# Attention, routed experts and a two-layer net: sink values loaded compactly and spread on chip, value maxima listed for ScalarE first

## The chip, the cores and the metric

The kernel runs on one core of one Trainium2 chip. The metric is the device time of one execution in microseconds (us), lower is better. Engines are named as in the profile: PE is TensorE (matmul), DVE is VectorE, ACT is ScalarE, POOL is GpSimd, SP is SyncE, which here only issues DMAs.

## The reference

Three stages follow one another. The first is attention with a sliding window of 128 keys and 4 "sink" keys, which every query sees:

```python
B, H, S, D = 2, 8, 768, 64
scores = scale * np.matmul(q, k.transpose(0, 1, 3, 2))
keep = is_sink | in_window
scores = np.where(keep, scores, -1000000000.0)
scores = scores - np.max(scores, axis=-1, keepdims=True)
a = np.exp(scores)
a = a / (np.sum(a, axis=-1, keepdims=True) + 1e-09)
return np.matmul(a, v).astype(np.float32)
```

The second routes 1536 tokens to 8 experts, 192 each, by a greedy order over all logits, and applies the expert's two layers (512 to 1024 to 512, with a relu). The third applies two dense layers (512 to 2048 to 512) with a leaky slope per column.

## The kernel before

**Planner.** The kernel does not write its instructions in the order of the loops. It lists tasks: each has an estimated duration for every engine that may run it, what it reads and what it writes. `Plan.run` then places them one after another: the task that can start first, and among those that can start together the one with the longest way to the end. Each engine runs its instructions in the order that comes out, so an instruction that waits on the chip holds up all that stands behind it on its engine. Where a task may run on two engines, the first one named is preferred: the other takes it only if it would be done earlier by a margin (`bias`, 0.85 us unless given). A changed estimate or preference can therefore move instructions anywhere in the stage.

**Attention.** Twelve blocks of 128 queries (6 per batch), each with four pairs of heads. For a pair: PE computes scores for two key blocks and four sink columns (line 485). DVE adds the mask and takes the row's extreme in one custom instruction (line 495, once per head). ACT takes the exponential into tile P (line 506, once per head). PE transposes P (line 520). ACT casts the transposed P to a 16-bit high part (line 529) and DVE subtracts it to get the low part (line 530). PE multiplies both with the values, which are also kept as a high part vh and a low part vl (lines 571 to 575). DVE divides by the row sums (lines 598 to 603).

**The values.** Four DMAs of three blocks each bring them to tile vraw. They are split in 16 bits after a scaling by a power of two, found from the largest absolute value over the six blocks of a batch. `vmax` takes the maximum of a block: on ACT as the sum of absolute values (line 407, an upper bound that serves as well), on DVE as a reduction (line 409). `BY_ACT` lists the blocks whose task names ACT first; for the others DVE is first. Behind six maxima stands a short chain of DVE and PE steps (`pow2_scale`, lines 388 to 396), which gives the scale svf. Only then can vh and vl be made, and only then can the first values product start.

**The sink values.** PE multiplies the probabilities of the sinks (tile sk, made by POOL at lines 539 to 541) with tile vsh, whose row for head h holds values only in the columns of head h and zeros elsewhere. Before the change that layout, zeros and all, is loaded from memory: vsr, 96 partitions by 2 x 2 x 8 x 65 numbers. `prep_vs` scales a batch of it on ACT (lines 454 and 455) and subtracts the high part on DVE in the low-part rows (line 458), over 1024 columns each time.

**Loads.** One queue on SP brings all inputs. `ORDER` names the order of the early ones: k and q of block 1, values a and b (blocks 0 to 2 and 3 to 5), the sink values s, the gate's weights w. The keys and queries of the later blocks and the other values follow.

**The end of the stage.** For each block the gate's logits are computed; the order of the 1536 tokens is then counted by comparing every token's best logit with every other's. The comparisons (tiles cm) are differences written by ACT (line 1121) or POOL (line 1123) and turned to 0 or 1 by DVE (lines 1127 and 1131), or made by DVE alone (line 1116). Blocks 0 to 8 are one group, blocks 9 to 11 a second, whose broadcast of logits (mrow, line 1100) needs the last block. PE sums them (line 1163), and the first expert follows. Everything from there on hangs on the end of that count.

## Time and profile before

| | us |
|---|---|
| median of 3 runs | 609.66 |
| lowest and highest of them | 609.23, 613.13 |
| the profiled execution, whole time | 608.75 |
| its span on the core | 607.0 |

The profile is of one execution. The span runs from its first to its last instruction; 1.75 us of its time lie around it. The attention stage with the count of tokens takes the first 119 us of the span. "Busy" is time in which an engine has at least one instruction; idle time is put down to what ended it. In rows by line, the mean is of one instruction, and instructions that overlap on an engine count once in its busy time.

### The profile page before, as it was taken

The page shows a single profiled execution, that of the slowest core. Times are in us where ns is not written, and L with a number is a line of the kernel's source. Part 1 is how long each engine was busy: PE and PEld are TensorE (multiplying, and loading weights), DVE is VectorE, ACT ScalarE, POOL GpSimd, SP SyncE. Part 2 cuts the span into 40 slices and gives each one's busy share as a digit, 9 for nine tenths or more (in the row PEclk, how much of TensorE's full clock was granted, in tenths as well). Part 3 has the DMA queues.
Part 4 walks back from the last instruction along what each step waited for, and adds up shares of the span by engine and source line. Part 5 has one row for each costly group of instructions (what it writes and reads, how often), then busy time and mean ns, then how long its engine had stood idle before and what let it go on. Part 6 is the DMA issues. An engine that isn't in the chain of part 4 may idle for free.

```text
span 607.0 us, 12432 instructions
## 1 busy us (share of the span) xinstructions
PE 559.9 (92%) x4532; PEld 410.0 (68%) x4532; DVE 461.2 (76%) x1299; ACT 357.7 (59%) x742; POOL 161.0 (27%) x247
## 2 busy tenths in 40 slices
PE   5899997659789999999899999999999999899995
PEld 3567675449688668888898555598755559855552
DVE  6989987858647898998699998989987657743231
ACT  6778888357457967866665553566344446542222
POOL 4867835230643321436301201000220000020002
PEclk9789998569889999999999999999999999999998
DMA  8845354264868536343554448464697155210001
GB/s 282 295 104 134 100 87 140 50 219 116 305 183 280 205 105 209 97 138 107 153 164 157 131 144 309 164 195 153 196 321 256 39 169 166 80 43 10 1 0 53
DMA packets 40555, 91.99 MB, mean 152 GB/s; under 512 B 16703, under 2 KB 17230, under 8 KB 40398
## 3 DMA queue, kind: packets, MB, share of 16 engines
q1 hardware_dynamic: 37710, 84.27, 44.3%
q0 software_dynamic: 2784, 6.93, 3.3%
q8 instruction: 36, 0.59, 0.4%
q14 instruction: 25, 0.20, 0.1%
HBM read 82.15 MB, written 6.41 MB: 146 GB/s over the span
## 4 chain that ended last, share of the span: by engine, by line
PE 47%; issue 12%; DVE 11%; ACT 8%; DMA 4%; POOL 1%; another core or an unknown queue 0%; POOLq 0%; SPq 0%; ACTq 0%
PE o L1751 14%; PE h L1708 13%; PE h L1574 8%; PE h L1581 8%; DMA xg<-xd,sidx 3%; DVE spl L1559 1%; DVE cm L1116 1%; PE r L1163 1%; DVE cm L1131 1%; ACT w L860 1%; PE r L1459 1%; ACT spl L1557 1%; ACT cm L1121 1%; DVE w L900 1%; DMA L<-cd 1%
## 5 line engine op out<-in xcount | busy, mean ns | idle before, releaser
L1751 PE MATMUL o<-w,gt 128*128 128x512 f16 x432 | 101.9, 379 | 0.0
L1708 PE MATMUL h<-x,w 128*128 128x384 f16 x576 | 100.7, 326 | 0.0
L1708 PEld LDWEIGHTS <-w 128*128 128x128 f16 x576 | 55.8, 98 | 40.6 <-issue 0.5
L1721 ACT ACTIVATE t<-h,slope 128x384 f32<-128x384 f32 x64 | 37.0, 578 | 72.3 <-PE h L1708 72.2
L1751 PEld LDWEIGHTS <-gt 128*128 128x128 f16 x432 | 41.3, 98 | 43.3 <-issue 0.5
L1581 PEld LDWEIGHTS <-spl 128*128 128x128 f16 x768 | 63.4, 98 | 3.2 <-issue 2.6
L1724 DVE SCALAR_TENSOR_TENSOR v<-h,way,t 128x384 f32<-128x384 f32 x61 | 37.3, 612 | 35.3 <-ACT t L1721 35.3
L907 POOL TENSOR_TENSOR w<-w,sg 128x512 f32<-128x512 f32 x22 | 28.8, 1310 | 88.8 <-DVE w L900 29.0
L1574 PE MATMUL h<-xT,raw 128*128 128x192 f32 x256 | 48.1, 338 | 2.3 <-DVE x L1625 1.8
L1446 POOL DMA_INDIRECT xg<-xd,sidx x16 | 20.6, 1286 | 100.5 <-DVE sidx L1440 62.4
L1574 PE MATMUL h<-h,raw 128*128 128x192 f32 x256 | 46.4, 339 | 0.4 <-DVE x L1625 0.4
L506 ACT ACTIVATE P<-sm,mn 128x260 f32<-128x260 f32 (+1 forms) x96 | 42.7, 491 | 4.7 <-DVE mn L495 4.6
L1797 POOL DMA_INDIRECT out<-ot,sidx x9 | 8.9, 990 | 136.2 <-ACT ot L1788 97.4
L1574 PEld LDWEIGHTS h<-xT,raw 128*128 128x128 f32 x256 | 42.5, 194 | 3.4 <-DVE x L1625 2.1
L1574 PEld LDWEIGHTS h<-h,raw 128*128 128x128 f32 x256 | 43.5, 198 | 1.1 <-DVE x L1625 0.6
L1559 DVE SCALAR_TENSOR_TENSOR spl<-raw,es,spl 128x1024 f16<-128x1024 f32 x32 | 40.7, 1280 | 4.5 <-ACT spl L1557 4.4
L1728 ACT CAST gt<-v 128x384 f16<-128x384 f32 x48 | 24.5, 510 | 28.9 <-DVE v L1724 27.5
L485 PE MATMUL s<-k,q 64*128 64x260 f32 (+1 forms) x192 | 36.8, 457 | 4.4 <-DMA q<-qT 4.1
L495 DVE CUSTOM_DVE_ANT_0 sm<-s,mask 128x260 f32<-128x260 f32 (+1 forms) x96 | 35.7, 397 | 4.1 <-PE s L485 3.8
L1729 DVE TENSOR_TENSOR gt<-v,gt 128x384 f16<-128x384 f32 x48 | 26.5, 553 | 13.7 <-ACT gt L1728 13.6
L1557 ACT ACTIVATE spl<-raw,es 128x1024 f16<-128x1024 f32 x32 | 36.4, 1143 | 0.0
L1581 PE MATMUL h<-xT,spl 128*128 128x192 f16 x384 | 33.5, 246 | 1.5 <-DVE h L1604 1.2
(291 smaller groups left out, 1241.5 us busy)
## 6 DMA issues: line engine op xcount, KB each, us to landing
raw<-w SPq DMA_DIRECT2D x96, 512.0 KB, 4.6
r<-w_in SPq DMA_DIRECT2D x16, 512.0 KB, 8.1
r<-w_out SPq DMA_DIRECT2D x16, 512.0 KB, 4.4
vraw<-v SPq DMA_DIRECT2D x4, 768.0 KB, 8.5
xd<-x SPq DMA_DIRECT2D x12, 256.0 KB
k<-kT SPq DMA_DIRECT2D x11, 260.0 KB
q<-qT SPq DMA_DIRECT2D x11, 256.0 KB, 2.8
vsr<-vs SPq DMA_DIRECT2D x1, 780.0 KB
```

Of the source, the lines that this page charges most:

```text
L485: nc.tensor.matmul(s.tile[:, :n].rearrange("p (j k) -> p j k", k=KW), lhsT=qs[t].tile[half, p], rhs=kk, start=True, stop=True)
L495: task({"DVE": dve(n)}, lambda: nc.vector.tensor_tensor_reduce(out=sm.tile[:, :n], in0=s.tile[:, :n], in1=mask[:, :n], scale=-0.125, scala ...
L506: task({"ACT": act(n) + 0.137}, lambda h=h, sm=sm, mn=mn: nc.scalar.activation(P[t].tile[:, h, :n], sm.tile[:, :n], AF.Exp, bias=mn.tile, ...
L907: (nc.gpsimd if e == "POOL" else nc.vector).tensor_tensor(x.tile, x.tile, sg.tile, OP.mult)
L1557: task({"ACT": act_sb(1024) + 0.09}, lambda: nc.scalar.activation(v(0), src(), AF.Copy, scale=scale()), r=[raw, ws], w=[b.part(0)], lag=se ...
L1559: task({"DVE": dve(1024) + 0.2}, lambda: nc.vector.scalar_tensor_tensor(v(1), src(), scale(), v(0), OP.mult, OP.subtract), r=[raw, ws, b.p ...
L1574: nc.tensor.matmul(ps.tile[:, 0:CAP], lhsT=w[:, k], rhs=x, start=first and k == 0, stop=last and k == 3, skip_group_check=True)
L1581: nc.tensor.matmul(ps.tile[:, 0:CAP], lhsT=w[:, i, k], rhs=xs()[k][:, j], start=first and n == 0, stop=last and n == len(ways) - 1, skip_g ...
L1708: nc.tensor.matmul(ps.tile[:, 0:CH], lhsT=w[:, i, k], rhs=y[j][:, k], start=(n == 0), stop=(n == len(ways) - 1))
L1721: task({"ACT": act(CH)}, lambda: nc.scalar.activation(t.tile, ps.tile[:, 0:CH], AF.Copy, scale=slope), r=[ps, wres], w=[t])
L1724: task({"DVE": dve(CH) + 0.065}, lambda: nc.vector.scalar_tensor_tensor(to(), ps.tile[:, 0:CH], way, t.tile, OP.mult, OP.max), r=[ps, t, w ...
L1751: nc.tensor.matmul(ops[t].tile, lhsT=gv[:, i, sl], rhs=wv[:, j], start=(f == n == 0), stop=(f == FB - 1 and n == 2))
```

## The change

Three things are done. `ORDER` puts the gate's weights ahead of the sink values. `BY_ACT` names all twelve blocks, so that each maximum has ACT as its preferred engine. The sink values come as vsr without the head dimension (96 x 260 numbers, 97.5 KB in place of 780 KB), are scaled and split at that size into vsd (ACT over 128 columns, DVE over 128), and are then spread over the heads by one multiplication of 96 x 1040 with a 0 or 1 mask named own; that task may run on POOL or on DVE. The mask is a reduction of the identity matrix on DVE.

```diff
--- before.py
+++ after.py
@@ -247,9 +247,9 @@
 TURNED = 2
 URGENT = 10.0
 EAGER = 40.0
-ORDER = "k q a b s w"
+ORDER = "k q a b w s"
 LATER = {2: (6, 9), 3: (9, 12)}
-BY_ACT = (0, 1, 3)
+BY_ACT = tuple(range(12))
 BIG = 1.0e30
 
 
@@ -292,7 +292,9 @@
     vraw = cst.tile([128, NBLK, DM], F32, name="vraw")
     kall = cst.tile([128, B, NB, NP, KW], F32, name="k")
     wgs = cst.tile([128, NP, E], F32, name="wgs")
-    vsr = cst.tile([96, B, 2, H, D + 1], F32, name="vsr")
+    vsr = cst.tile([96, B, 2, D + 1], F32, name="vsr")
+    vsd = cst.tile([96, B, 2, D + 1], F16, name="vsd")
+    own = cst.tile([96, H], F16, name="own")
     vsh = cst.tile([96, B, 2, H, D + 1], F16, name="vsh")
     wg16 = cst.tile([128, 2, NP, E], F16, name="wg16")
     mx = cst.tile([128, NBLK], F32, name="mx")
@@ -333,7 +335,7 @@
         load(lambda: nc.sync.dma_start(out=wgs, in_=wg), [wg_res], 1 << 14)
 
     def load_vs():
-        load(lambda: nc.sync.dma_start(out=vsr, in_=vs), [vs_res], 1 << 19)
+        load(lambda: nc.sync.dma_start(out=vsr, in_=vs), [vs_res], 1 << 17)
 
     for x in ORDER.split():
         {"a": lambda: load_v(0, 3), "b": lambda: load_v(3, 6), "c": lambda: load_v(6, 9), "d": lambda: load_v(9, 12),
@@ -345,6 +347,9 @@
         if t in LATER:
             load_v(*LATER[t])
 
+    own_res = Res()
+    task({"DVE": 0.2}, lambda: nc.vector.tensor_reduce(
+        own, ident[0:96, 0:96].rearrange("p (r h x) -> p h r x", r=3, h=H), AX.XY, OP.max), w=[own_res])
     warm = cst.tile([128, 1], F32, name="warm")
     nc.vector.memset(warm, 0.0)
     nc.scalar.activation(warm, warm, AF.Exp)
@@ -451,13 +456,22 @@
 
     def prep_vs(b):
         def first():
-            nc.scalar.activation(vsh[:, b, :, :, 0:D], vsr[:, b, :, :, 0:D], AF.Copy, scale=svf[b][0:96])
-            nc.scalar.copy(vsh[:, b, :, :, D:D + 1], vsr[:, b, :, :, D:D + 1])
-
-        task({"ACT": 1.1}, first, r=[vs_res, sv_res[b]], w=[vsh_res[b]])
-        task({"DVE": 1.15}, lambda: nc.vector.scalar_tensor_tensor(
-            vsh[64:96, b, :, :, 0:D], vsr[64:96, b, :, :, 0:D], svf[b][64:96], vsh[64:96, b, :, :, 0:D],
-            OP.mult, OP.subtract), r=[vs_res, sv_res[b]], w=[vsh_res[b]])
+            nc.scalar.activation(vsd[:, b, :, 0:D], vsr[:, b, :, 0:D], AF.Copy, scale=svf[b][0:96])
+            nc.scalar.copy(vsd[:, b, :, D:D + 1], vsr[:, b, :, D:D + 1])
+
+        def rest():
+            nc.vector.scalar_tensor_tensor(vsd[64:96, b, :, 0:D], vsr[64:96, b, :, 0:D], svf[b][64:96], vsd[64:96, b, :, 0:D],
+                                           OP.mult, OP.subtract)
+
+        def spread(e):
+            (nc.vector if e == "DVE" else nc.gpsimd).tensor_tensor(
+                vsh[:, b], vsd[:, b].unsqueeze(2).to_broadcast([96, 2, H, D + 1]),
+                own.unsqueeze(1).unsqueeze(3).to_broadcast([96, 2, H, D + 1]), OP.mult)
+
+        dense = Res()
+        task({"ACT": 0.4}, first, r=[vs_res, sv_res[b]], w=[dense])
+        task({"DVE": 0.25}, rest, r=[vs_res, sv_res[b]], w=[dense])
+        task({"POOL": 2.3, "DVE": 1.2}, spread, r=[dense, own_res], w=[vsh_res[b]])
 
     def geo(t):
         b, i = divmod(block(t), NB)
@@ -724,17 +738,17 @@
         kT[:, j, ..., 128:] = kt[:, 0, ..., 2 * g:2 * g + 2]
     a["kT"] = kT.reshape(NBLK, 128, NP, KW)
     a["v"] = np.ascontiguousarray(v.reshape(B, H, NB, 128, D).transpose(3, 0, 2, 1, 4)).reshape(128, NBLK, DM)
-    vs = np.zeros((3, H, 2, 2, B, 2, H, D + 1), v.dtype)
+    vs = np.zeros((3, H, 2, 2, B, 2, D + 1), v.dtype)
     for r in range(3):
         for par in range(2):
             for g in range(2):
                 for s in range(2):
                     n = 2 * ((g + par + 1) % 2) + s
                     for h in range(H):
-                        vs[r, h, g, s, :, par, h, :D] = v[:, h, n, :]
+                        vs[r, h, g, s, :, par, :D] = v[:, h, n, :]
                         if r < 2:
-                            vs[r, h, g, s, :, par, h, D] = 1
-    a["vs"] = vs.reshape(96, B, 2, H, D + 1)
+                            vs[r, h, g, s, :, par, D] = 1
+    a["vs"] = vs.reshape(96, B, 2, D + 1)
     wg = np.asarray(inputs["moe_w_gate"])
     a["wg"] = np.ascontiguousarray(wg.reshape(NP, 128, E).transpose(1, 0, 2))
     return a
```

Below are three places in the program where the instructions of before and of the changed kernel differ. Line numbers of the changed kernel are 2 to 14 higher.

First, ACT behind the first exponential of block 1. P is written by an exponential, pth by a cast of transposed P; junk, mx is the maximum of a block of values. Before:

```order
L407 ACTIVATE junk,mx<-vraw 128x512 x2
L506 ACTIVATE P_340<-sm_334,mn_335 128x260
L506 ACTIVATE P_340<-sm_342,mn_343 128x260
L506 ACTIVATE P_340<-sm_352,mn_353 128x260
L407 ACTIVATE junk,mx<-vraw 128x512
L529 CAST pth_383<-pt_337 128x256
L506 ACTIVATE P_340<-sm_362,mn_363 128x260
L506 ACTIVATE P_340<-sm_366,mn_367 128x260
L529 CAST pth_396<-pt_369 128x256
L506 ACTIVATE P_340<-sm_375,mn_376 128x260
L506 ACTIVATE P_340<-sm_386,mn_387 128x260
L529 CAST pth_413<-pt_402 128x512
```

In the changed kernel:

```order
L412 ACTIVATE junk,mx<-vraw 128x512 x3
L520 ACTIVATE P_343<-sm_337,mn_338 128x260
L412 ACTIVATE junk,mx<-vraw 128x512 x3
L520 ACTIVATE P_343<-sm_345,mn_346 128x260
L520 ACTIVATE P_343<-sm_353,mn_354 128x260
L543 CAST pth_412<-pt_340 128x256
L520 ACTIVATE P_343<-sm_363,mn_364 128x260
L520 ACTIVATE P_343<-sm_366,mn_367 128x260
L543 CAST pth_432<-pt_369 128x256
L520 ACTIVATE P_343<-sm_376,mn_377 128x260
L412 ACTIVATE junk,mx<-vraw 128x512 x3
L445 ACTIVATE vh_230<-vraw,scv_161 128x8x64
```

Before, two maxima and later one stand between the exponentials here. Now there are three, three and three, and the last three follow a few rows on, so that all twelve are on ACT. The high part vh of block 0, the step that the first values product needs, stands behind nine of them, where it stood behind three.

Second, DVE at the end of the stage, around the last two tiles xT (the last two blocks' outputs, transposed and split). Before:

```order
L621 SCALAR_TENSOR_TENSOR xT_2359<-pt_2306,scv_165,xT_2359 128x512
L601 TENSOR_SCALAR r_2377<-pv_2347,scv_165 128x4
L603 RECIPROCAL r_2377<-r_2377 128x4
L598 TENSOR_TENSOR x_2354<-pv_2347,r_2377 128x256
L621 SCALAR_TENSOR_TENSOR xT_2407<-pt_2400,scv_165,xT_2407 128x512
L1127 TENSOR_TENSOR cm_2311<-cm_2311,trih 128x128
L1131 TENSOR_SCALAR cm_2311<-cm_2311 128x1024
L1127 TENSOR_TENSOR cm_2328<-cm_2328,trih 128x128
L1131 TENSOR_SCALAR cm_2328<-cm_2328 128x128
L1131 TENSOR_SCALAR cm_2328<-cm_2328 128x896
L1127 TENSOR_TENSOR cm_2344<-cm_2344,trih 128x128
L1067 TENSOR_REDUCE m_2234<-L 128x3
```

In the changed kernel:

```order
L1141 TENSOR_TENSOR cm_2313<-cm_2313,trih 128x128
L615 TENSOR_SCALAR r_2377<-pv_2359,scv_167 128x4
L617 RECIPROCAL r_2377<-r_2377 128x4
L612 TENSOR_TENSOR x_2357<-pv_2359,r_2377 128x256
L635 SCALAR_TENSOR_TENSOR xT_2375<-pt_2346,scv_167,xT_2375 128x512
L1145 TENSOR_SCALAR cm_2313<-cm_2313 128x1024
L1141 TENSOR_TENSOR cm_2326<-cm_2326,trih 128x128
L1145 TENSOR_SCALAR cm_2326<-cm_2326 128x128
L1145 TENSOR_SCALAR cm_2326<-cm_2326 128x896
L1141 TENSOR_TENSOR cm_2353<-cm_2353,trih 128x128
L1145 TENSOR_SCALAR cm_2353<-cm_2353 128x256
L635 SCALAR_TENSOR_TENSOR xT_2411<-pt_2388,scv_167,xT_2411 128x512
```

The last xT stood ahead of all the work on cm; now seven instructions on cm stand ahead of it.

Third, POOL at the last of the differences cm. Before:

```order
L1123 TENSOR_SCALAR cm_2394<-mrow,m_2234 128x384
L1123 TENSOR_SCALAR cm_2397<-mrow,m_2234 128x896
L1123 TENSOR_SCALAR cm_2409<-mrow,m_2234 128x1024
L1123 TENSOR_SCALAR cm_2476<-mrow,m_2234 128x256
L1123 TENSOR_SCALAR cm_2491<-mrow,m_2234 128x1408
L1445 MEMSET xg_2763 64x512
L1446 DMA xg_2794<-xd,sidx_2788 128x512
```

In the changed kernel:

```order
L1137 TENSOR_SCALAR cm_2383<-mrow,m_2251 128x512
L1137 TENSOR_SCALAR cm_2393<-mrow,m_2251 128x384
L1137 TENSOR_SCALAR cm_2428<-mrow,m_2251 128x256
L1137 TENSOR_SCALAR cm_2441<-mrow,m_2251 128x1024
L1459 MEMSET xg_2768 64x512
L1460 DMA xg_2799<-xd,sidx_2793 128x512
```

The two pieces of the second group (256 and 1408 columns) are no longer on POOL; ACT has them. The spreading of the sink values is not on POOL either: both of its instructions (`L467 TENSOR_TENSOR vsh<-vsd,own 96x1040`) stand on DVE.

## Rows read from the trace of the kernel before

**Rows 1.** The page, part 1: busy us, share of span, instructions.

```profile
PE 559.9 (92%) x4532; PEld 410.0 (68%) x4532; DVE 461.2 (76%) x1299; ACT 357.7 (59%) x742; POOL 161.0 (27%) x247
```

**Rows 2.** Stretches: length, busy us (instructions) of each engine, granted clock, DMA share.

```profile
9.70:23.30 13.60, 10.95 (x92) 7.07 (x89) 12.98 (x48) 11.23 (x27) 6.95 (x11) 0.87 1.03 366
23.30:34.00 10.70, 9.15 (x67) 5.59 (x63) 9.69 (x37) 7.44 (x15) 6.20 (x9) 0.68 0.42 115
...
34.00:64.00 30.00, 28.86 (x387) 20.80 (x387) 28.11 (x110) 25.63 (x60) 21.62 (x39) 1.00 0.52 133
64.00:94.00 30.00, 29.36 (x437) 21.99 (x436) 27.24 (x113) 26.97 (x67) 17.80 (x29) 1.00 0.42 90
94.00:108.80 14.80, 10.23 (x177) 8.27 (x175) 11.51 (x52) 13.07 (x26) 9.78 (x11) 0.77 0.41 125
```

**Rows 3.** Groups by line, 0 to 110 us: busy us, mean ns, idle.

```profile
L506 ACT ACTIVATE P<-sm,mn 128x260 f32<-128x260 f32 (+1 forms) x96 | 42.7, 491 | 4.7 <-DVE mn L495 4.6
...
L495 DVE CUSTOM_DVE_ANT_0 sm<-s,mask 128x260 f32<-128x260 f32 (+1 forms) x96 | 35.7, 397 | 4.1 <-PE s L485 3.8
...
L530 DVE TENSOR_TENSOR ptl<-pt,pth 128x512 f16<-128x512 f32 (+1 forms) x48 | 30.5, 636 | 1.6 <-ACT pth L529 1.5
L529 ACT CAST pth<-pt 128x512 f16<-128x512 f32 (+1 forms) x48 | 25.9, 540 | 4.1 <-PE pt L520 3.1 <-PE pv L573 0.7
...
L409 DVE TENSOR_REDUCE mx<-vraw 128x1 f32<-128x512 f32 x8 | 5.1, 676 | 0.0
...
L458 DVE SCALAR_TENSOR_TENSOR vsh<-vsr,scv,vsh 32x1024 f16<-32x1024 f32 x2 | 2.6, 1315 | 0.1
L407 ACT ACTIVATE junk<-vraw 128x512 f32<-128x512 f32 x4 | 2.5, 621 | 0.0
...
L454 ACT ACTIVATE vsh<-vsr,scv 96x1024 f16<-96x1024 f32 x2 | 2.3, 1152 | 0.9 <-DVE scv L390 0.9
```

**Rows 4.** Timeline, 9 to 34 us: start, length, engine, line, operation.

```profile
9.71 0.62 ACT L407 ACTIVATE junk<-vraw 128x512 f32<-128x512 f32 x1
...
10.45 0.63 ACT L407 ACTIVATE junk<-vraw 128x512 f32<-128x512 f32 x1
...
16.34 0.72 ACT L440 ACTIVATE vh<-vraw,scv 128x512 f16<-128x512 f32 x1
...
12.77 1.28 DVE L409 TENSOR_REDUCE mx<-vraw 128x1 f32<-128x512 f32 x2
...
19.64 0.26 PE L571 MATMUL pv<-vh,pth 128*128 128x65 f16 x1
```

**Rows 5.** Waits of SP's queue, 0 to 60 us: total, times, longest.

```profile
SPq L317 <- DMA vsr<-vs: 2.7, 1, 2.7
```

**Rows 6.** As rows 3: rows near to the new small operations.

```profile
L1131 DVE TENSOR_SCALAR cm<-cm 128x1024 bf16<-128x1024 bf16 (+7 forms) x16 | 4.4, 305 | 0.0
...
L550 ACT COPY skt<-pv 96x128 f16<-96x128 f16 x8 | 2.1, 260 | 5.6 <-PE pv L548 3.0 <-DVE r L601 1.5 <-DVE x L598 1.1
...
L1127 DVE TENSOR_TENSOR cm<-cm,trih 128x128 bf16<-128x128 bf16 x9 | 2.0, 218 | 0.0
```

**Rows 7.** Timeline, 22 to 45 us, and POOL's group of line 539.

```profile
29.37 1.28 DVE L458 SCALAR_TENSOR_TENSOR vsh<-vsr,scv,vsh 32x1024 f16<-32x1024 f32 x1
...
30.05 0.67 POOL L539 TENSOR_SCALAR sk<-P 128x32 f16<-128x32 f32 x1 [1.48 <-ACT P L506]
...
L539 POOL TENSOR_SCALAR sk<-P 128x32 f16<-128x32 f32 x7 | 2.2, 317 | 2.3 <-ACT P L506 2.2
```

**Rows 8.** End of stage: DVE timeline, chain that ended last, POOL groups.

```profile
102.51 0.75 DVE L621 SCALAR_TENSOR_TENSOR xT<-pt,scv,xT 128x512 f16<-128x512 f32 x1 [1.89 <-ACT xT L619]
...
109.07 1.31 issue
110.38 2.38 DVE cm L1116 x7
...
L1123 POOL TENSOR_SCALAR cm<-mrow,m 128x256 bf16<-128x256 f32 x1 | 2.7, 2674 | 3.0 <-ACT mrow L1100 3.0
```

## The prediction

> **What bounds the kernel now.** I read the page's busy times first. PE is busy 92% of the span [rows 1], and the change adds and removes no product, so a gain can only come from a stage in which PE waits for others. The change touches the attention stage alone; behind it stand instructions in the same order as before. The second view is therefore busy time by stretch of that stage [rows 2]. DVE is busy 12.98 of 13.60 us between 9.7 and 23.3, 9.69 of 10.70 up to 34, then 28.11 and 27.24 of 30: idle 0.6, 1.0, 1.9 and 2.8 us. ACT is idle 2.4, 3.3, 4.4 and 3.0 us. PE reads as busy as DVE from 34 on. The Trainium skill's page Trainium Kernel Development and Optimization, section Performance Expectations, calls matmul busy time a bad measure, because matmuls are pipelined; here the weight loads next to it are busy 20.80 and 21.99 of 30 [rows 2], which agrees with it. So DVE is the bound of the stage, with ACT second. In the last stretch that turns: ACT is busy 13.07 of 14.80 and DVE 11.51 [rows 2], and DVE waits 1.89 us for ACT before the last xT [rows 8].
>
> The third view is the groups by line [rows 3]. Their busy time over their count is what one costs its engine: mask and maximum of scores 35.7/96 = 0.37 us and low part 30.5/48 = 0.64 on DVE; exponential 42.7/96 = 0.44 and cast 25.9/48 = 0.54 on ACT; a maximum of values 5.1/8 = 0.64 on DVE. On ACT a maximum is 0.62 long, but two in a row start 0.74 apart [rows 4], so a run of three is 0.74 + 0.74 + 0.63 = 2.1.
>
> **The load.** 682 KB less on the one queue. A later k load waits 2.7 us for vsr before it is even issued [rows 5], so later inputs come up to 2.7 us earlier. But the idle times of rows 3 were ended by DVE, PE and ACT, none by a load. I cost it at nothing; it covers the maxima, which read the third group of values earlier than the sinks are needed. The other end is that 2.7, should the new order on ACT read values sooner than they would have come.
>
> **The engines' sums.** DVE loses eight maxima, 8 x 0.64 = 5.1, and two low parts over 1024 columns, 2.6 [rows 3]. It gains two low parts over 128 columns, 0.22 each by the nearest row [rows 6], and two spreadings over 1040 columns, since the order shows none on POOL. No row shows such an operation. Twice the columns of the low part at line 530 cannot cost less than its 0.64; eight times line 1127's 0.218 makes 1.8 [rows 3, 6]; line 458 has two inputs and 1024 columns and takes 1.3 [rows 3]. I take 1.3, so 2.6 for both (1.3 to 3.5). The mask own, about 0.2 by line 1127, falls where DVE still waits for the first scores (4.1 us of idle before line 495 [rows 3]). Net for DVE: -5.1 - 2.6 + 0.4 + 2.6 = -4.7 (-6.0 to -3.8).
>
> ACT gains eight maxima: four runs of 2.1 are 8.4, against about 2.7 for the four of before, +5.7. It loses two sink scalings, 2.3 [rows 3], for two over 128 columns, which I put at 0.4 each (0.26 by line 550 [rows 6], 0.54 by a cast). Net +4.2.
>
> **Where that falls: the start.** This is where I chose. ACT has 2.4 + 3.3 = 5.6 us of idle between 9.7 and 34 [rows 2], and gets 5.7 of maxima there, so it becomes full. From the first maximum at 9.71 on: three maxima, an exponential, three maxima end at 9.71 + 2.1 + 0.44 + 2.1 = 14.35 (before, the sixth ended on DVE at 12.77 + 1.28 = 14.05 [rows 4]). Then five exponentials, two casts of half width (0.3 each) and three more maxima: 14.35 + 2.2 + 0.6 + 2.1 = 19.25. Only now comes vh of block 0, ending at 19.9 instead of 17.06 [rows 4]. With vl on DVE behind it (0.64, as line 530), the first values product starts at about 20.6 instead of 19.64 [rows 4]: 1.0 us late. On DVE 24 maxima of scores stand ahead of the first division by row sums, where 18 stood, and the gate's weights are split ahead of it, which they were behind it (two small steps, 0.4 by line 1127). DVE has room for these as six maxima of values are gone from there. So at that point it is 1.0 us later but 6 x 0.37 + 0.4 = 2.6 further: 1.6 ahead. Two maxima of values less to come are 1.3; the sink steps to come are 0.4 dearer (3.0 against 2.6). Lead: 1.6 + 1.3 - 0.4 = 2.5. From there DVE bounds and ACT, with 10 us of idle to 94, can make up its backlog. But the work done ahead is only the scores' half, and the exponentials that free its tiles are on the full ACT, so I keep 2.4 (0 to 4.7, the whole relief).
>
> **The end.** Seven cm instructions now stand ahead of the last xT, where DVE idled 1.89 us [rows 8]. By lines 1131 and 1127 they are 4 x 0.28 + 3 x 0.22 = 1.8; they overlap in part, so 1.3 goes into the gap (0 to 1.8). Second, in the chain that ended last, one step at line 1116 waits 1.31 us where the next seven take 2.38, 0.34 each [rows 8]; at that time a POOL piece of only 256 columns takes 2.67 us [rows 8]. I read this as both engines held up by each other. That POOL piece and its partner are gone, to ACT; ACT takes some 1800 columns more, at an exponential's 0.44 per 260 at most 3.0 us, late enough to eat a part. I take 1.0 (0 to 1.3).
>
> Sum: 2.4 + 1.3 + 1.0 = 4.7. The profiled execution took 608.75 in all (607.0 of span); 608.75 - 4.7 = 604.1 us. It lies 0.9 under the median of 609.66. What follows the stage is a chain (routing, first gather), so I let the gain pass whole.
>
> **Rivals.**
> First, slower: ACT becomes the bound and stays it. What speaks for it: vh of block 0 is 2.8 us late, ACT's idle of 5.6 is spent to the last, and that idle was waits for DVE and PE which need not vanish; the granted clock was 0.68 between 23.3 and 34 [rows 2], so partly at 1.2 GHz, and a PE left waiting at 15 to 20 us could run there longer. Against: DVE loses its bound at the same time. It decides once DVE waits over 3 us for ACT or PE between 10 and 34. Price: 1.0 for the late product up to the net 4.2 of ACT, say 3: 611.8 us.
>
> Second, the port between DVE and POOL. A POOL step on sk took 0.67 us, usually 0.32, and ended at 30.72, just behind a two-input DVE step that ran from 29.37 to 30.65 [rows 7]. The Trainium skill's page SBUF — State Buffer, section Who interferes with whom, has the rule: a DVE instruction with two SBUF inputs and a GpSimd one that reads SBUF exclude each other for a whole instruction. The rows agree. The spreadings are such steps, as were those they replace; new is that seven cm steps on DVE now run while POOL still makes its differences. Two collisions of about 1.2 each, as in rows 8, undo the gain at the end: 608.75 - 2.4 = 606.3 us.
>
> Third, no gain: PE bounds after all (28.86 and 29.36 busy of 30 [rows 2]). Then at most its idle of 1.8 between 34 and 94 can be had, say half: 607.9 us. Against it stand the weight loads.
>
> Fourth, the whole relief arrives: 4.7 + 1.8 + 1.3 = 7.8, or 601.0 us.
>
> That the change doesn't do what it says is half shown already: the spreading isn't on POOL; it is in the sum so.
>
> **How the numbers follow.** Forecast 0.50, first rival 0.12, second 0.13, third 0.17, fourth 0.08. Range 600.5 to 610.5: from just under the fourth to within the first, whose upper half is left out. A measurement of this kernel can tell about 1%, 6.1 us, from no change. Faster by more: all of the fourth and that part of the forecast in which the start gives over 3.8, 0.22, together 0.30. Slower by more: the upper part of the first, and what I have not seen, 0.10. Between: 0.60.
>
> **What would show it.** Right: DVE busy some 4.7 us less up to the count's end, ACT some 4 more; first values product at 20 to 21.5 us; DVE waiting for ACT at 10 to 24 but under 3 us; no idle of 1.9 before the last xT, no DVE step of line 1116's kind of 1.5 us; the count of tokens, and each later stage, 4 to 5 us earlier. Wrong: vh of block 0 past 22 us, or ACT still the releaser of DVE after 34; a spreading over 1.8 us; POOL pieces of 1 us and more beside DVE steps on cm; or a stage behind the count that takes back the lead.

## The result, and the profile after

The changed kernel took 606.39 us (median of 22 runs, 599.74 to 611.39) where the kernel before took 610.88 in the same comparison (22 runs, 606.47 to 615.79). The ratio is 0.9917, 95% interval 0.9894 to 0.9939: 0.83% or 5.1 us less. The ratio leaves out runs that lie over 1.5% above the fastest of their kernel (609.70 and 611.39 of the changed one), so it is not that of the two medians. A second comparison on another chip, where the kernel before takes 603, gave 0.9935 (0.9909 to 0.9960), 3.9 us less. The forecast was 4.7 less than the profiled execution of before, 604.1 us. So the size came out; the terms it was made of did not all.

The profiled execution of the changed kernel took 607.93 us (span 606.2), 1.5 above its median. First its busy times, from part 1 of the page, to be read against [rows 1].

```profile
PE 560.5 (92%) x4531; PEld 411.4 (68%) x4532; DVE 457.8 (76%) x1294; ACT 364.5 (60%) x760; POOL 157.9 (26%) x245
```

DVE lost 3.4 us and ACT gained 6.8. The same stretches as in [rows 2] (length, busy us of PE, PEld, DVE, ACT and POOL with instructions, granted clock, DMA share, GB/s):

```profile
9.70:23.30 13.60, 11.85 (x50) 6.63 (x50) 8.48 (x45) 12.41 (x34) 2.74 (x7) 0.83 0.90 343
23.30:34.00 10.70, 9.29 (x97) 6.54 (x94) 9.01 (x37) 7.52 (x19) 8.75 (x13) 0.74 0.38 102
34.00:64.00 30.00, 27.41 (x379) 20.59 (x380) 28.06 (x102) 26.82 (x64) 21.39 (x37) 1.00 0.42 124
64.00:94.00 30.00, 28.81 (x415) 21.91 (x414) 27.82 (x115) 27.27 (x65) 18.48 (x31) 1.00 0.36 90
94.00:108.80 14.80, 10.46 (x193) 8.98 (x191) 13.44 (x53) 12.98 (x29) 8.67 (x11) 0.84 0.47 144
```

Two stretches differ. In the first, DVE is busy 8.48 of 13.60 us, before 12.98: it no longer bounds the start, and ACT is close to full. In the last, DVE is busy 13.44 instead of 11.51: the hole at the end is filled. The 8.48 is the lowest of the four profiles of the changed kernel's start in the table below (8.5 to 9.2), the 12.98 the highest of the four of the kernel before (10.8 to 13.0). The groups by line up to 110 us, as [rows 3]:

```profile
L509 DVE CUSTOM_DVE_ANT_0 sm<-s,mask 128x260 f32<-128x260 f32 (+1 forms) x96 | 35.5, 397 | 9.2 <-PE s L499 9.0
...
L412 ACT ACTIVATE junk<-vraw 128x512 f32<-128x512 f32 x12 | 7.5, 626 | 0.3
L467 DVE TENSOR_TENSOR vsh<-vsd,own 96x1040 f16<-96x1040 f16 x2 | 2.7, 1356 | 0.0
...
L463 DVE SCALAR_TENSOR_TENSOR vsd<-vsr,scv,vsd 32x128 f16<-32x128 f32 x2 | 0.9, 456 | 0.1
```

All twelve maxima are on ACT. DVE's wait for scores, ahead of the mask and maximum, went from 3.8 us [rows 3] to 9.0: what DVE no longer has to do at the start is waited away there. The four profiles of each kernel in the table below have 3.8 to 5.5 and 6.4 to 9.0. Where, the timeline shows (start, length, engine, line, operation, idle before and its releaser; as [rows 4]):

```profile
8.80 1.24 PE L499 MATMUL s<-k,q 64*128 64x260 f32 x4 [1.29 <-DMA q<-qT]
...
11.37 0.62 ACT L412 ACTIVATE junk<-vraw 128x512 f32<-128x512 f32 x1
...
20.69 0.71 ACT L445 ACTIVATE vh<-vraw,scv 128x512 f16<-128x512 f32 x1
...
22.13 2.10 PE L499 MATMUL s<-k,q 64*128 64x260 f32 x8
...
23.51 0.43 DVE L509 CUSTOM_DVE_ANT_0 sm<-s,mask 128x260 f32<-128x260 f32 x1 [1.54 <-PE s L499]
...
23.86 1.15 DVE L447 SCALAR_TENSOR_TENSOR vl<-vraw,scv,vh 128x512 f16<-128x512 f32 x1
...
24.17 0.24 PE L585 MATMUL pv<-vh,pth 128*128 128x65 f16 x1
...
25.07 0.21 PE L587 MATMUL pv<-vl,pth 128*128 128x64 f16 x1 [0.66 <-DVE vl L447]
```

The first values product starts at 24.17, 4.5 us later than in [rows 4]; 1.7 of this is there at the first maximum already (11.37 against 9.71; the block of queries came late), and eight score products stand right ahead of it on PE. The second one waits 0.66 us for vl, which DVE starts only at 23.86, behind a maximum of scores that waited 1.54 us for the same score products. At the end of the stage DVE's timeline reads (as [rows 8]):

```profile
102.08 0.75 DVE L635 SCALAR_TENSOR_TENSOR xT<-pt,scv,xT 128x512 f16<-128x512 f32 x1
102.75 0.78 DVE L1145 TENSOR_SCALAR cm<-cm 128x1024 bf16<-128x1024 bf16 x1
...
103.58 0.68 DVE L1145 TENSOR_SCALAR cm<-cm 128x128 bf16<-128x128 bf16 x2
...
104.32 1.06 DVE L1145 TENSOR_SCALAR cm<-cm 128x256 bf16<-128x256 bf16 x1
105.30 0.74 DVE L635 SCALAR_TENSOR_TENSOR xT<-pt,scv,xT 128x512 f16<-128x512 f32 x1
...
109.76 3.05 DVE L1130 TENSOR_SCALAR cm<-mrow,m 128x384 bf16<-128x384 f32 x9
...
119.09 0.16 DVE L1222 SCALAR_TENSOR_TENSOR dead<-rk,dead 128x12 f32<-128x12 f32 x1
```

The last xT is 2.8 us later than in [rows 8] (105.30, 102.51), but no idle time stands ahead of it, and the nine pieces at line 1130 (line 1116 before) take 3.05 us. The dead flags of the first count, with which the stage's work ends, come at 119.09; in the kernel before at 119.05. By this one pair the stage gained nothing. That is why most of the runs below also show how much two executions of one kernel differ.

### The profile page after: what moved, and what is told of

Same layout as the page of the kernel before. It is cut to its first block, busy times and chain, and to the rows that moved or that the text cites. A ratio compares the mean times of both kernels' runs of the same rounds, so it can differ in the third digit from the quotient of the medians.

```text
span 606.2 us, 12439 instructions
## 1 busy us (share of the span) xinstructions
PE 560.5 (92%) x4531; PEld 411.4 (68%) x4532; DVE 457.8 (76%) x1294; ACT 364.5 (60%) x760; POOL 157.9 (26%) x245
## 4 chain that ended last, share of the span: by engine, by line
PE 48%; issue 12%; DVE 10%; ACT 7%; DMA 3%; POOL 2%; another core or an unknown queue 1%; POOLq 0%; SPq 0%; ACTq 0%
PE o L1765 14%; PE h L1722 13%; PE h L1588 9%; PE h L1595 8%; DMA xg<-xd,sidx 3%; DVE spl L1573 1%; PE r L1177 1%; ACT w L874 1%; PE r L1473 1%; ACT spl L1571 1%; ACT cm L1135 1%; DVE cm L1130 1%; DVE w L914 1%; DVE ohs L1280 1%; DMA L<-cd 1%
## 5 line engine op out<-in xcount | busy, mean ns | idle before, releaser
L1588 PE MATMUL h<-xT,raw 128*128 128x192 f32 x256 | 50.3, 347 | 2.9 <-ACT h L1622 2.6
L1588 PEld LDWEIGHTS h<-xT,raw 128*128 128x128 f32 x256 | 44.1, 200 | 4.6 <-ACT h L1622 3.3
L1460 POOL DMA_INDIRECT xg<-xd,sidx x16 | 20.6, 1287 | 100.0 <-DVE sidx L1454 62.4
L1588 PEld LDWEIGHTS h<-h,raw 128*128 128x128 f32 x256 | 42.2, 193 | 2.3 <-ACT xf L1633 0.8
L499 PE MATMUL s<-k,q 64*128 64x260 f32 (+1 forms) x192 | 35.4, 464 | 5.4 <-DMA q<-qT 5.4
L1571 ACT ACTIVATE spl<-raw,es 128x1024 f16<-128x1024 f32 x32 | 36.4, 1142 | 0.0
L534 PE MATMUL pt<-ident,P 128*128 128x128 f32 x176 | 31.0, 299 | 4.6 <-DVE ptl L544 3.0
```

The source lines that it names most:

```text
L499: nc.tensor.matmul(s.tile[:, :n].rearrange("p (j k) -> p j k", k=KW), lhsT=qs[t].tile[half, p], rhs=kk, start=True, stop=True)
L534: nc.tensor.transpose(o[:, a, g], P[t].tile[:, 2 * p + a, g * KW:g * KW + 128], ident)
L1571: task({"ACT": act_sb(1024) + 0.09}, lambda: nc.scalar.activation(v(0), src(), AF.Copy, scale=scale()), r=[raw, ws], w=[b.part(0)], lag=se ...
L1588: nc.tensor.matmul(ps.tile[:, 0:CAP], lhsT=w[:, k], rhs=x, start=first and k == 0, stop=last and k == 3, skip_group_check=True)
```

## The experiments

Two places are read in every profile: the last xT, and the dead flags. What lies between them I call the closing. It was 16.5 us in each of three profiles of the kernel before, and 13.79 in each of three of the changed kernel. The ratios below are to the kernel before, run in the same group.

**More profiles of both kernels.** No edit; two more profiles of the kernel before, one of the changed kernel, and the changed kernel timed again with a profile of its own.

> The kernel before once more, for a second profile. If the late start of the changed kernel's profile (first maximum on ACT at 11.37 instead of 9.71, TensorE at the lower clock from about 8 us) is a matter of the execution and not of the change, some profiles of this kernel show it too, with the first values product 2 us or more behind 19.64. If it belongs to the change, this profile starts as the first one did, within 0.5 us.

> The changed kernel once more, for a second profile. If its late start is a matter of the execution, this profile has its first maximum near 9.7 and its first values product at 20 to 21.5 us as forecast, and the last xT and all behind it 3 to 5 us earlier than in the first profile, with an execution near 604. If it belongs to the change, the first maximum stands at 11 us or later again and the first values product near 24.

> The changed kernel again, on one chip with the kernels of this group. Two pairs of profiles show the last xT of the attention stage 0.5 and 2.8 us later than before, and from there to the dead flags of the count 13.8 us instead of 16.5. Theory one (the gain is the closing 2.75 us less what the start loses): 0 to 2.5 us faster than before. Theory two (the first comparison, 0.9917, is the size of it): 4 to 6 us faster, and then part of it must lie where these profiles do not show it.

> The kernel before once more for its profile: last xT against the first maximum on ACT (92.8 and 93.7 us in its first two profiles, 93.7 to 94.3 in those of the changed kernel). Within 0.7 us of 93.3: the start and the middle of the change give nothing in time. At 95 or more: they do give 1 us or more, and the first two profiles were early ones.

Start of the instruction in us; the last column of each half is a kernel from below whose work is the same up to the last xT.

| | before | again | third | end on ACT | after | again | rounds | end on POOL |
|---|---|---|---|---|---|---|---|---|
| first maximum on ACT | 9.71 | 9.93 | 10.23 | 10.49 | 11.37 | 9.75 | 10.41 | 10.01 |
| first values product | 19.64 | 21.14 | 22.55 | 22.76 | 24.17 | 22.46 | 23.55 | 22.81 |
| last xT | 102.51 | 103.58 | 107.96 | 105.62 | 105.30 | 104.03 | 104.65 | 105.40 |
| dead flags | 119.05 | 120.10 | 124.48 | 120.72 | 119.09 | 117.82 | 118.44 | 120.64 |

The late first maximum belongs to the execution (9.75 in the second profile). The first product is later with the change: 23.2 us in the mean of four against 21.5, so 1.7, of which 0.3 is the first maximum. Counted from the first maximum it comes at 12.9 against 11.4, and the two kernels' profiles do not mix (12.7 to 13.1, 9.9 to 12.3). From the first product to the last xT the changed kernel needs 81.6 us in the mean, the kernel before 83.4, so 1.8 are regained, and the last xT comes at 104.8 and 104.9 in the means. 0.7 of these 1.8 come from one execution of the kernel before, the third, which lost some 2.7 us in the middle: without it the kernel before needs 82.7, and 1.1 is regained. Its stretch from 34 to 64 shows a lower granted clock than [rows 2]:

```profile
34.00:64.00 30.00, 28.76 (x355) 21.00 (x355) 26.52 (x100) 23.92 (x56) 19.15 (x34) 0.89 0.48 104
```

The other three of the kernel before read 1.00, 0.99 and 1.00 there, those of the changed kernel 1.00, 0.94, 1.00 and 0.94; among the profiles at 0.99 or 1.00 alone, 1.6 is regained.

The second profiles fell between the cases set for them: the kernel before has its first product 1.5 us behind 19.64, and the changed kernel has it at 22.46, with the last xT 1.3 us earlier than in its first profile. The changed kernel timed again, at 3.9 us less, lies between its two theories (0 to 2.5 and 4 to 6). The third profile of the kernel before fell on the side "95 or more" (107.96 - 10.23 = 97.7), but the other profiles do not bear out a gain in start and middle: 0.1 us between means whose members lie up to 5.5 us apart. Behind the dead flags both kernels do the same work. To the end of the span they take 480.2 and 480.1 us in the second profiles, which are from one chip, and 488.0 and 487.1 in the first ones. But the other profiles scatter: the kernel before and its variants have 480.0 to 480.3, the changed kernel timed again has 478.7, and its variants with the end on POOL and with doubled scores (both below) have 482.7 and 480.9. Why, no run shows.

**The kernel before, without POOL's pieces in the second group.**

```diff
-seq.append(task({"ACT": act_sb(n), "POOL": n * 1.0e-3 + 0.02},
+seq.append(task({"ACT": act_sb(n)} if s == 0 and a else {"ACT": act_sb(n), "POOL": n * 1.0e-3 + 0.02},
```

> The kernel before with one edit: the differences over the second group's columns (blocks 9 to 11) may stand on ACT only, so the POOL piece of 256 columns and the one of 1408 are gone. My theory (POOL's piece and the DVE steps at line 1116 hold each other up for 1.0 us): no DVE step of line 1116 with 1.3 us or more of waiting ahead, the closing (last xT to dead flags) 15.5 instead of 16.5, the time 1.0 us lower. Rival (the pieces only move, ACT ends the stage with 1800 columns more): closing 16.5 or longer, time the same or 1 to 2 us higher.

Ratio 0.9979 (0.9953 to 1.0006), 1.3 us less, which by its interval could still be no change. DVE's timeline has the nine pieces at

```profile
111.38 3.04 DVE L1116 TENSOR_SCALAR cm<-mrow,m 128x384 bf16<-128x384 f32 x9
```

instead of, in the kernel before,

```profile
108.39 4.37 DVE L1116 TENSOR_SCALAR cm<-mrow,m 128x384 bf16<-128x384 f32 x9
```

(the wait of 1.31 us in [rows 8] falls within these), and the closing is 15.10. ACT now has five pieces there, 4.88 us, and does not end the stage.

**The changed kernel, with these pieces put back on POOL.**

```diff
-seq.append(task({"ACT": act_sb(n), "POOL": n * 1.0e-3 + 0.02},
+seq.append(task({"POOL": n * 1.0e-3 + 0.02} if s == 0 and a and (c1, x) in ((9, 1280), (10, 0))
+                else {"ACT": act_sb(n), "POOL": n * 1.0e-3 + 0.02},
```

> The changed kernel with the two pieces of the second group's columns (256 and 1408) put back on POOL. My theory (their absence is worth 1.0 us): closing 14.8 instead of 13.8 us, time 1 us above the changed kernel of the same group. Rival (the closing is shorter only because the cm steps stand ahead of the last xT): closing 13.8, time the same; then the fill was worth 2.75 alone.

Ratio 0.9957 (0.9925 to 0.9988), 1.3 us above the changed kernel of the group, with intervals that overlap. The timeline of DVE, then of POOL:

```profile
109.90 4.37 DVE L1130 TENSOR_SCALAR cm<-mrow,m 128x384 bf16<-128x384 f32 x9
```

```profile
108.94 2.81 POOL L1137 TENSOR_SCALAR cm<-mrow,m 128x256 bf16<-128x256 f32 x2 [3.53 <-DVE cm L1145]
```

The stall of 1.3 us is back with the two POOL pieces beside it, and the closing is 15.24. Two kernels, one edit in either direction, 1.43 and 1.45 us in the rows: this term is shown by the rows; the two times move the same way by 1.3 us each, which is within their noise. The other half of the closing's gain, 15.10 to 13.79, fits the seven cm steps that now stand ahead of the last xT, which take DVE 1.36 us behind it in the kernel before (103.18 to 104.54); no run moved them alone.

**Each half of the change alone.** First the sinks (the maxima as before), then the maxima (the sinks as before).

```diff
-BY_ACT = tuple(range(12))
+BY_ACT = (0, 1, 3)
```

> The sink half of the change alone: 97 KB of sinks, scaled small and spread on DVE; maxima on ACT for groups 0, 1 and 3 only, as before. My theory (the gain is DVE's relief by eight maxima, 5.1 us): DVE is relieved of two low parts (2.6 us) and gets two spreadings of 1.24 and 1.48 us, two small low parts and the mask, so its sum stays within 0.7 us and the time within 1 us of before; ACT has 1.5 us more room. Rival (the shorter load counts, the later loads come up to 2.7 us earlier): 2 to 3 us faster than before, and the first scores' waits for DMA shorter.

Ratio 0.9998 (0.9970 to 1.0026): within 1 us of before, as my theory said, but not for its reason. DVE's sum to the dead flags is 104.5 us (before 102.7), 1.8 more where at most 0.7 was expected. The rival's 2 to 3 us from the shorter load did not show. The closing is 13.56 already, with the nine pieces undisturbed:

```profile
110.55 3.05 DVE L1130 TENSOR_SCALAR cm<-mrow,m 128x384 bf16<-128x384 f32 x9 [0.25 <-ACT mrow L1114]
```

but the last xT comes at 106.99, later than in three of the four profiles of the kernel before. In this one profile the longer work of DVE takes what the closing gives.

```diff
-BY_ACT = (0, 1, 3)
+BY_ACT = tuple(range(12))
```

> The maxima half alone: all maxima of values prefer ACT (eleven stand there), the sinks as before. My theory: DVE loses 5.1 us of maxima, the start gives about 2.4 and the gap before the last xT 1.3, while the POOL pieces over second-group columns stay, so the 1.0 at the end is not had: 3 to 4 us faster than before, and slower than the whole change by 1 to 2. Rival one (ACT is the bound at the start, its two sink scalings still 1.1 us each): within 1 us of before or slower, with DVE waiting over 3 us for PE or ACT between 10 and 34. Rival two (the gain needs the small load): within 1 us of before.

Ratio 1.0030 (1.0002 to 1.0057), 1.8 us slower where I expected 3 to 4 faster: a miss. DVE's sum falls to 100.5, and the last xT, at 103.20, is not late. But the order of the end is the old one and POOL has more in it; the closing is 17.29, with a cm step of 128 columns held for 1.01 us (0.21 elsewhere) and the nine pieces for 4.37:

```profile
103.20 0.75 DVE L621 SCALAR_TENSOR_TENSOR xT<-pt,scv,xT 128x512 f16<-128x512 f32 x1 [1.96 <-ACT xT L619]
103.87 1.01 DVE L1127 TENSOR_TENSOR cm<-cm,trih 128x128 bf16<-128x128 bf16 x1
...
109.84 4.37 DVE L1116 TENSOR_SCALAR cm<-mrow,m 128x384 bf16<-128x384 f32 x9
```

Rival one had named a time like this; its condition is on the line (between 10 and 34 us DVE waits 3.0 us for PE, 2.2 of it for scores). The closing, 0.8 us longer than before, explains less than half of the 1.8; behind the dead flags this profile has 481.2 us, before 480.0 to 480.3.

The halves, 0 and +1.8, do not add up to -4 or -5. The idle time of 1.96 ahead of the last xT and the stall went only where the sink half had changed the planner's order, and DVE's relief came only with the maxima. That the two need each other is read from these rows; no run shows it by itself.

**Is TensorE the bound at the start?** The scores of the third block are computed twice, in the changed kernel and in the kernel before.

```diff
+for _ in range(2 if t == 2 else 1):
     nc.tensor.matmul(s.tile[:, :n].rearrange("p (j k) -> p j k", k=KW), lhsT=qs[t].tile[half, p], rhs=kk, start=True, stop=True)
```

> The changed kernel with the scores of the third block computed twice: four more groups of products on TensorE (0.71 us each at the better pace in these traces, 1.24 at the worse, so 2.8 to 5.0 us), all of them ahead of the first values product; no other engine gets an instruction. Theory one (with all six maxima ahead of vh and 24 maxima of scores ahead of the first division, the start of the changed kernel hangs on TensorE: DVE waits 8 to 9 us for scores up to the count, before 3.9): the first values product and the last xT come 3 to 5 us later against the first maximum, the time 3 to 5 us longer than the changed kernel. Theory two (TensorE only waits at the start and has room): under 1 us.

> The same doubling in the kernel before. Theory one: fewer of these scores stand ahead of the first values product there and DVE, not TensorE, is the bound, so less of the 2.8 to 5.0 us comes through than in the changed kernel, 1 to 2.5 us. Theory two (TensorE has room): under 1 us. If as much comes through as in the changed kernel, TensorE bounds the start of both, and the change has not moved the bound.

Ratios 0.9949 (0.9919 to 0.9979) and 1.0013 (0.9990 to 1.0035): 0.8 us above the changed kernel's 0.9935 and 0.8 above the kernel before. Theory one expected 3 to 5 and 1 to 2.5. The first does not fit (the interval ends 2.7 us above 0.9935), the second is not ruled out (it ends 2.1 us above the kernel before). PE's timeline shows why the doubling could cost so little; first the profile with the doubling, then the changed kernel as it is:

```profile
16.26 2.13 PE L500 MATMUL s<-k,q 64*128 64x260 f32 x16
...
21.12 1.59 PE L500 MATMUL s<-k,q 64*128 64x260 f32 x12
```

```profile
15.50 2.11 PE L499 MATMUL s<-k,q 64*128 64x260 f32 x8
...
21.51 2.10 PE L499 MATMUL s<-k,q 64*128 64x260 f32 x8
```

Sixteen products took what eight did. PE ran at twice the pace in that execution, from 14.35 us on and so before the first doubled product; whether the doubling kept it there or the execution was lucky, one profile can't tell. In sum all score products up to the count took 36.3 us for 208 and 36.4 for 192. With the doubling the first product even stands nearer to the first maximum, at 11.3 us (12.7 to 13.1 in the changed kernel), and the last xT still does not come earlier (94.6 us behind the first maximum, 93.9 to 95.4 in the changed kernel). So PE has room at the faster pace; what the doubled products cost at the slower one is not shown.

**Fewer maxima ahead of the first vh.** The changed kernel with maxima 2, 4 and 5 on DVE as before.

```diff
-BY_ACT = tuple(range(12))
+BY_ACT = (0, 1, 3, 6, 7, 8, 9, 10, 11)
```

> The changed kernel, but of the first six groups of values three maxima (2, 4, 5) stay on DVE, as before; the last six go to ACT. If the changed kernel loses at the start because six maxima in front of vh leave TensorE without work (its clock 0.50 from 16 us, DVE waiting 3.7 us and more for scores), this one has the first values product near 20 us, DVE waits under 2 us for TensorE between 10 and 24, and it is 1 to 3 us faster than the changed kernel. Rival (the start's order does not decide, the sums of DVE do): 1.9 us more on DVE (three maxima), so the same or up to 2 us slower than the changed kernel.

Ratio 0.9941 (0.9917 to 0.9964), the changed kernel's 0.9935 within its interval. DVE's wait for scores between 9 and 34 us fell to 1.7 us (4.4 in the changed kernel of the group), as expected, and in its one profile the last xT comes at 102.22; but the first product stands at 22.97, not near 20, and the time is the same. The edit did not bring vh forward: the planner set three maxima of the second batch right ahead of it, and vh ends 11.4 us after the first maximum, later than in the changed kernel (10.0 to 10.3):

```profile
20.54 0.63 ACT L412 ACTIVATE junk<-vraw 128x512 f32<-128x512 f32 x1
...
21.17 0.71 ACT L445 ACTIVATE vh<-vraw,scv 128x512 f16<-128x512 f32 x1
```

The planner also put the two spreadings on POOL here, which takes 2.7 us from DVE. With both in it, the run does not say whether the maxima ahead of vh decide. The second leads to the last kernel.

**The spreadings on POOL alone.**

```diff
-task({"POOL": 2.3, "DVE": 1.2}, spread, r=[dense, own_res], w=[vsh_res[b]])
+task({"POOL": 2.3}, spread, r=[dense, own_res], w=[vsh_res[b]])
```

> The changed kernel with the two spreadings on POOL alone (1.92 us each there, in the kernel that split the first maxima; on DVE 1.24 and 1.48). If DVE's sum bounds from the first division on, 2.7 us less on DVE bring the last xT 1 to 2.5 us earlier and the time 1 to 2 us below the changed kernel. Rival (the POOL step holds the port against DVE, or delays POOL's low parts of values for which TensorE waits): the same time or up to 2 us longer.

Ratio 0.9906 (0.9878 to 0.9934), the lowest of all, 5.7 us under the kernel before. Its busy times to the dead flags, below those of the changed kernel (columns as in the stretches):

```profile
0.00:116.91 116.91, 99.30 (x1239) 73.22 (x1239) 96.92 (x416) 97.81 (x229) 68.30 (x137) 0.93 0.50 147
```

```profile
0.00:118.44 118.44, 99.33 (x1238) 72.06 (x1239) 99.61 (x419) 97.54 (x227) 68.04 (x137) 0.94 0.49 145
```

DVE is busy 2.7 us less and the dead flags come 1.5 earlier. A spreading takes POOL 1.92 us, yet POOL's sum stays (68.30, 68.04): two cm pieces went from POOL to ACT, and POOL's 22 steps on vh and vraw are shorter (0.70 us instead of 0.77 each). So here too the planner changed the order, and the spreading is not the only difference. Against the changed kernel (0.9935 and 0.9917) the gain is 0.7 to 1.7 us, but the intervals overlap: that this kernel beats the kernel before is shown, that it beats the changed one is not.

## Why the prediction was right, and where it was not

**The sum.** -4.7 us was forecast; -5.1 and -3.9 were measured. Within 1% of before, as the likeliest case said. The time itself, 606.39, lies 2.3 us above the forecast of 604.1, because the profiled execution it was worked from lies 2.1 under the median of 22 runs (608.75, 610.88). That the size came out is in part luck: the 2.4 from the start is not found in the profiles, which show 0.1, and the end gave more than its 2.3.

**The end: right, and mis-sized by half a microsecond.** The two terms were 1.3 for cm steps in the idle time ahead of the last xT and 1.0 for the hold-up between POOL's piece and the pieces at line 1116, together 2.3. The closing gave 2.74 (16.53 to 13.79): 1.3 and 1.45. The hold-up was taken at 1.0 of at most 1.3; it is the whole step and a little more. What rival two had said of the port happened beside it: in the changed kernel the cm steps ahead of the last xT are stretched (0.78, 0.68 and 1.06 us above, where the kernel before has 0.42, 0.49 and 0.22), 1.4 us in sum, while POOL works on its pieces of the first group, one of which takes 1.40 us where their median is 0.70. These were named as a sign of being wrong. In the kernel before:

```profile
103.31 0.42 DVE L1131 TENSOR_SCALAR cm<-cm 128x1024 bf16<-128x1024 bf16 x1
...
103.78 0.49 DVE L1131 TENSOR_SCALAR cm<-cm 128x128 bf16<-128x128 bf16 x2
...
104.41 0.22 DVE L1131 TENSOR_SCALAR cm<-cm 128x256 bf16<-128x256 bf16 x1
```

The stretch had a price: xT's first half on ACT was ready at 104.33, 0.97 us before DVE took the last xT up at 105.30.

```profile
103.61 0.72 ACT L633 ACTIVATE xT<-pt,scv 128x512 f16<-128x512 f32 x1
```

It did not undo the gain, because with six of the seven steps between them the last two xT still stand no further apart than before (3.22 us, before 3.44), and the closing is rid of these steps. The stretched steps have one input. I had taken the rule from the Trainium skill's page SBUF — State Buffer, section Who interferes with whom, for instructions with two SBUF inputs; the same section also names tensor_scalar in its two-port modes as taking the pair of ports for a whole instruction, and these rows agree with that. In three of the runs (the maxima alone, fewer maxima ahead of vh, the spreadings on POOL) the step held is one with two inputs (line 1127 or 1141), at 1.01, 0.97 and 0.96 us instead of 0.21.

**The start: the step that failed.** The time of vh was right: it ends 10.0 to 10.3 us after the first maximum, forecast 10.2. The failed step is "With vl on DVE behind it (0.64, as line 530), the first values product starts at about 20.6". The product came 2.7 to 2.9 us behind the end of vh, not 0.7. The lag could be read in [rows 4]: 2.6 us in the kernel before (17.06 to 19.64), and 2.9 to 3.0 in its other three profiles. There vl is done in time, and PE's own queue is what stands ahead of the product:

```profile
17.38 0.93 DVE L442 SCALAR_TENSOR_TENSOR vl<-vraw,scv,vh 128x512 f16<-128x512 f32 x1
...
18.73 1.12 PE L520 MATMUL pt<-ident,P 128*128 128x128 f32 x4
...
19.71 0.24 PE L573 MATMUL pv<-vl,pth 128*128 128x64 f16 x1
```

In the changed kernel PE's queue holds the product (22.13 to 24.23 above), and vl does not follow vh: it starts 2.5 us behind it, after maxima of scores that wait for PE, takes 1.15 us where 0.64 was set down (the row above has 0.93), and holds the second product 0.9 us behind the first (0.07 in the kernel before). What the change made later is vh: it ends 10.1 us after the first maximum in the mean of four, 8.6 in the kernel before. So the 1.0 for the late product came out near the measured 1.4 (from the first maximum) by two errors that met: vh was set 2.8 late against the earliest of four profiles, where the means are 1.5 apart, and the lag behind it was taken 2 us too short.

The lead was wrong too. I had counted what DVE runs ahead, 24 maxima of scores instead of 18, and called the difference a lead; the same 24 need their score products on PE first. So DVE waits 6.4 to 9.0 us for scores instead of 3.8 to 5.5, 3.5 more in the mean. The lead of 2.4 was forecast as 3.4 regained less 1.0 lost; in the profiles it is 1.8 regained (1.1 or 1.6 if profiles at a lower clock are left out as above) less 1.7 lost. The condition of the first rival, DVE waiting over 3 us for ACT or PE between 10 and 34, was met (5.5 us for scores in the first profile, 3.7 in the other three), and its loss did not come: ACT was not the bound afterwards, and the relief of DVE made good what the start lost. The point of decision was set wrongly.

**The engines' sums.** To the dead flags DVE has 99.5 to 99.8 us instead of 102.7 and 102.8 (104.2 in the third profile of the kernel before), so -3.1; forecast -4.7, with -3.8 as the end of the range. The parts named came to -3.9: the spreadings 2.7 (forecast 2.6), the small low parts 0.9 (0.4), the mask own 0.2 as said. The stretched cm steps (+1.5) and vl (+0.2) are made good by the nine undisturbed pieces (-1.3) and the gate's low part (0.25 us, before 0.67), so 0.8 of the difference stays without a name. ACT has 6.6 us more, forecast 4.2 and up to 3.0 for the columns at the end; these alone are 2.4 in the kernel before with its end on ACT (93.3, 90.9). The spreading took 1.24 us once in each profile, 1.47, 1.48 and 2.08 the other time (over 1.8 was a sign of being wrong); the scaling on ACT 0.40, as taken.

**What stays open.** The times ask for 1 to 2 us from start and middle (3.9 or 5.1, less 3.0 of the end, counted from the last xT but one); the profiles show 0.1, from four and four whose means are good to about a microsecond. Both can hold, and a part can lie behind the dead flags, where the profiles of the changed kernel and its variants lie up to 4 us apart. The third rival's price, at most 0.9 us, is out by both times. PE as the bound of the middle was not tested: the doubled products stand at the start. That DVE bounds the middle fits the last kernel, where the dead flags come 1.5 us earlier with 2.7 less work on DVE, but one pair of profiles with a changed order does not show it.

## What to carry to other kernels

Work taken from the bound engine gains only from the point where that engine bounds; at the start, count for each instruction that moves ahead what the other in-order queues must run first, PE's too, and where the profile of before already shows a lag, take the lag from there. Where two engines hold each other up, look for the pair of rows (a short piece that takes several times its usual length, and a step beside it) and take either one away: that was the surest part of this change, and one edit in the kernel before has half of it. Where a planner orders the rest, time each half of a change before saying which one paid: here neither did by itself.

## What the runs showed of the hardware

Score products on PE run at two paces, four of 260 columns in 0.71 us (the row below, from the second profile of the changed kernel) or in 1.24 (at 8.80 in its first), and the granted clock of a stretch does not always tell which: in the changed kernel timed again it reads 1.00 (2.4 GHz) from 9.7 to 34 us while groups of eight take 2.1 us, and in the doubled one, also at 1.00, sixteen take 2.13. In the first profile of the changed kernel, the stretch from 8 to 16 us, which an expectation calls the lower clock, also reads 1.00. At which pace PE runs changes from one execution to the next. The latest last xT of the kernel before, 5.5 us behind the earliest, is in the execution that reads 0.66 from 34 to 44 us and 0.89 from 34 to 64; that this is the reason is likely and not shown.

```profile
24.14 0.71 PE L499 MATMUL s<-k,q 64*128 64x260 f32 x4
```

The hold-up between POOL and DVE has one size. The nine pieces on DVE at line 1116 or 1130 took 4.36 or 4.37 us in the six profiles with POOL's two pieces beside them, and 3.04 or 3.05 in the eight without: 1.32 us, whether those two took POOL 4.18, 5.49 or 2.81 us.
